# One DMA per block across two batches for x and its reciprocal sums, in a fused attention and two-layer kernel on one Trainium2 core

## The chip, the core and the metric

The kernel runs on one core of one Trainium2 chip as one program. The metric is the time of one execution on the device in microseconds (us), the median over several runs. A profile of one further execution was taken by the hardware profiler. Engines are called PE (matrix products), ACT, DVE and POOL (elementwise work) and SP (which here only issues DMAs).

## The reference, cut to what matters

```python
# q, k, v: 4 batches, 8 heads, 576 positions, 64 wide; x below: 2304 tokens x 512
scores = scale * np.matmul(q, k.transpose(0, 1, 3, 2))
thresh = np.max(scores, axis=-1, keepdims=True) - tau
scores = np.where(scores >= thresh, scores, -1000000000.0)
attn = np.exp(scores - np.max(scores, axis=-1, keepdims=True))
attn = attn / (np.sum(attn, axis=-1, keepdims=True) + 1e-09)
x = heads_side_by_side(np.matmul(attn, v))
g = x @ w_gate                                   # 512 -> 1536
x = (g * (1.0 / (1.0 + np.exp(-g))) * (x @ w_val)) @ w_out
out = ((x @ w1) * (x @ w2) @ w3) @ w_out2        # 512 -> 1024 -> 1024 -> 512
```

## The kernel before

Matrix products are made of two float32 halves: each operand is rounded to a high part (a cast on ACT), a low part is the difference (a subtraction on DVE, helper `sub`, L1545), and three products of the halves (`PASSES`, helper `mm3`, L1505) replace one.

The first stage, attention, goes over 16 pairs of heads (4 batches of 4 pairs). It leaves two things in DRAM. `x_dram` holds the value products, not yet divided by the sums: two partial results (first axis) by 512 features by 4 batches by 576 positions. Each pair of heads stores its 2 x 64 features of a batch (L899, and L1350 for the last two pairs). `r_dram` holds the reciprocals of the softmax sums as high and low halves, for 4 batches and 8 heads (`r_store`, L693 to L702).

The second stage works on 2304 tokens, batch after batch, in five blocks of 512, 512, 256, 512 and 512 columns (`blocks`, numbers 0 to 4). A batch has 576 positions, so blocks 1, 2 and 3 each lie over the end of a batch: block 1 has 64 columns of batch 0 and 448 of batch 1, block 2 has 128 and 128, block 3 has 448 and 64. `segs` cuts a block at these ends. `x_block` (L1846) brings a block in. Its sums come by two DMAs for each piece (L1857), one for each half of the heads. For each of four groups of 128 features (kk) one DMA for each piece (L1871) brings both partial results, POOL adds them (L1879), PE spreads the reciprocals over 128 partitions by a small product with a 0/1 matrix (`spread`, L1887), DVE multiplies (L1895), ACT takes the high half (L1899) and DVE the low half (L1545). Blocks 3 and 4 keep the multiplied value too (ACT, L1904). The spreads of block 0 go to banks `T` (four of one bank each), those of the other blocks to banks `S` (two of two banks each, so two spreads fill one, and the next pair needs the other).

Then `plain` (L1783) makes the first three column groups f of the gate and value products for all blocks, 24 matrix products per block and f on PE (in four groups of three, twice), a silu on ACT (L1806), a multiply on DVE (L1815) and a store of h (L1818). Later groups use a seven-product scheme (`seven`, L1712). Weights are unpacked from 64-bit words beside it (L422, L423 on ACT; L1587, L1590, L1595, L1599, L1601 on DVE).

The end of attention runs in the same span as the start of the second stage: the last pair's probabilities are turned on PE (L587) and split into `AT` and `ATL` by POOL (L367, L372) or by ACT and DVE (L1297, which frees a bank `T` when it is done), and the value products follow (L1327 and L1332, in banks `T`), whose results ACT copies and SP stores.

The order of every engine's instructions is fixed before the run by a planner (`Program.order`, L194). Each step has an engine, how long it keeps it (`busy`), after what time its result is seen (`until`), the buffers that it reads and writes, and a due number. The planner replays all queues with these costs, and of the steps that can start soonest it takes the one with the smallest due number. So a changed cost of one step can change the places of others on all engines. SP's queue is strictly in order: an issue that waits holds all later ones. The costs that `x_block` gives are 1.2 for each piece of the sums and 0.55 for each piece of an x load.

## Time and profile before

| what | value |
|---|---|
| median of 3 runs | 1075.82 us (1075.81, 1075.82, 1083.23) |
| the profiled execution | 1077.25 us |
| its span, from first to last instruction | 1075.5 us |
| instructions | 17044 |
| granted clock of PE, mean | 0.994 of full speed |
| DMA | 162.37 MB, 151 GB/s in the mean |

The profiled execution's time holds its span and 1.75 us around it. The granted clock is at full speed in every stretch that this case is about. The views used below are the busy time by stretch, and the timeline of single engines, in which a row gives the start, the duration (of all instructions that it merges, where xN stands at its end), the engine, the source line, what is written and read, and in brackets how long the engine stood idle before it and which instruction released it.

### The profile page before, as it was taken

To read this page: it belongs to the slowest core of one execution; us is meant where nothing else is said; L and a number is where in the kernel's file an instruction comes from. 1 tells how busy PE (TensorE), PEld (TensorE's weight loads), DVE (VectorE), ACT (ScalarE), POOL (GpSimd) and SP (SyncE) were. 2 spreads that over 40 slices of the span, in tenths; PEclk is the share of its full clock that TensorE was granted. 3 is DMA by queue.
4 is the path that set the end of the run, shared out by engine and by line. 5 is a ranking of instruction groups with operands and counts; after the bars stand their busy time and mean duration, and the time that the engine had idled before them with its cause. 6 is when DMAs were issued, how large, how long until landed. Compare 5 with 4: busy or idle time off the path is not lost.

```text
span 1075.5 us, 17044 instructions
## 1 busy us (share of the span) xinstructions
PE 1046.3 (97%) x5834; PEld 909.8 (85%) x5834; DVE 851.3 (79%) x1680; ACT 632.3 (59%) x1288; POOL 284.7 (26%) x307
## 2 busy tenths in 40 slices
PE   7999999999999999999999999999999999999998
PEld 6898898999977888888888889878888888888886
DVE  7999999999998879999999975976977776442320
ACT  5898898998975546665667654544433444232220
POOL 4799898997865000000000000000000000000000
PEclk8999999999999999999999999999999999999999
DMA  7686867765557124546456661461222325621531
GB/s 181 145 219 166 198 168 176 189 169 145 152 155 252 70 99 159 181 154 204 155 181 238 226 230 41 157 234 40 84 84 89 122 92 193 240 79 53 150 121 49
DMA packets 127206, 162.37 MB, mean 151 GB/s; under 512 B 48688, under 2 KB 83312, under 8 KB 127120
## 3 DMA queue, kind: packets, MB, share of 16 engines
q1 hardware_dynamic: 126976, 161.29, 49.9%
q8 instruction: 46, 0.75, 0.3%
q14 instruction: 40, 0.33, 0.1%
q10 hardware_dynamic: 144, 0.00, 0.0%
HBM read 93.47 MB, written 44.19 MB: 128 GB/s over the span
## 4 chain that ended last, share of the span: by engine, by line
PE 72%; DVE 17%; DMA 3%; issue 3%; ACT 2%; POOL 2%; SPq 1%; DVEq 0%; ACTq 0%; POOLq 0%
PE t_bank L1505 26%; PE t_bank L1705 16%; PE s_bank L1705 11%; PE s_bank L1505 6%; PE s_bank L623 5%; DVE E L655 3%; DVE P L671 3%; PE t_bank L865 3%; PE t_bank L587 3%; DVE slot L1545 3%; POOL AT L372 1%; PE t_bank L877 1%; DVE stat L664 1%; DMA slot<-v_dram 1%; DMA slot<-x_dram 1%
## 5 line engine op out<-in xcount | busy, mean ns | idle before, releaser
L1505 PE MATMUL t_bank<-slot,slot 128*128 128x512 f32 (+1 forms) x1680 | 339.2, 360 | 2.5 <-DVE slot L1545 2.5
L1505 PEld LDWEIGHTS t_bank<-slot,slot 128*128 128x128 f32 x1680 | 284.0, 189 | 53.2 <-DVE slot L1545 4.4
L1705 PE MATMUL t_bank<-slot,slot 128*128 128x512 f32 x816 | 196.7, 390 | 0.9 <-ACT tmp L1724 0.9
L1545 DVE TENSOR_TENSOR slot<-slot,slot 128x512 fp32r<-128x512 f32 (+1 forms) x247 | 157.4, 672 | 40.4 <-ACT slot L1996 27.1
L1705 PEld LDWEIGHTS t_bank<-slot,slot 128*128 128x128 f32 x816 | 152.0, 188 | 32.4 <-ACT tmp L1724 1.6
L1705 PE MATMUL s_bank<-slot,slot 128*128 128x512 f32 x612 | 147.0, 389 | 0.0
L372 POOL TENSOR_TENSOR AT<-tmp,AT 128x512 fp32r<-128x512 f32 x105 | 136.6, 1310 | 3.8
L1705 PEld LDWEIGHTS s_bank<-slot,slot 128*128 128x128 f32 x612 | 114.9, 188 | 23.8
L1724 ACT COPY tmp<-t_bank 128x512 f32<-128x512 f32 x102 | 59.3, 583 | 114.0 <-PE t_bank L1705 113.9
L680 ACT ACTIVATE P<-P,stat 128x576 f32<-128x576 f32 x144 | 113.8, 795 | 6.5 <-DVE P L671 6.3
L671 DVE SCALAR_TENSOR_TENSOR P<-E,stat,s_bank 128x576 f32<-128x576 f32 x144 | 114.4, 809 | 1.7
L1553 ACT CAST slot<-slot 128x512 fp32r<-128x512 f32 x135 | 81.1, 621 | 52.2 <-DVE slot L1545 21.3
L623 PE MATMUL s_bank<-R,L 128*128 128x288 f32 x512 | 95.3, 310 | 12.7 <-DVE P L671 9.9
L655 DVE TENSOR_SCALAR_CACHE_REDUCE E<-s_bank 128x576 f32<-128x576 f32 x135 | 100.5, 753 | 8.1 <-PE s_bank L623 7.3
L623 PEld LDWEIGHTS s_bank<-R,L 128*128 128x128 f32 x512 | 74.6, 191 | 20.8 <-DVE P L671 7.2
L587 PE MATMUL t_bank<-ident,P 128*128 128x128 f32 x640 | 89.1, 274 | 0.5 <-ACT tmp L797 0.2
L1505 PE MATMUL s_bank<-slot,slot 128*128 128x512 f32 (+1 forms) x432 | 84.7, 354 | 0.0
L1505 PEld LDWEIGHTS s_bank<-slot,slot 128*128 128x128 f32 x432 | 71.5, 189 | 11.3
L865 PE MATMUL t_bank<-AT,sp 128*128 128x288 f32 x448 | 76.9, 304 | 0.5 <-POOL AT L372 0.5
L422 ACT ACTIVATE raw<-raw,ebias 128x512 int32<-128x512 int32 x76 | 58.8, 774 | 31.3 <-DVE slot L1595 29.4
L587 PEld LDWEIGHTS t_bank<-ident,P 128*128 128x128 f32 x640 | 74.5, 141 | 3.2 <-ACT tmp L797 0.7
L367 POOL TENSOR_SCALAR AT<-tmp 128x512 fp32r<-128x512 f32 x105 | 66.3, 638 | 31.4 <-ACT tmp L797 26.1
(159 smaller groups left out, 1339.3 us busy)
## 6 DMA issues: line engine op xcount, KB each, us to landing
slot<-h_dram SPq DMA_DIRECT2D x40, 512.0 KB
h_dram<-h SPq DMA_DIRECT2D x34, 512.0 KB
raw<-in_moe_w_dram SPq DMA_DIRECT2D x32, 512.0 KB
raw<-in_moe_w_out_dram SPq DMA_DIRECT2D x20, 512.0 KB
x_dram<-xs SPq DMA_DIRECT2D x64, 144.0 KB
L<-qlo SPq DMA_DIRECT2D x60, 128.0 KB
L<-qhi SPq DMA_DIRECT2D x60, 128.0 KB
raw<-in_moe_w_gate_dram SPq DMA_DIRECT2D x12, 512.0 KB
```

Of the source, the lines that this page charges most:

```text
L367: nc.gpsimd.tensor_scalar(out=hi, in0=src, scalar1=1.0, scalar2=1.0, op0=ALU.mult, op1=ALU.mult)
L372: nc.gpsimd.tensor_tensor(out=lo, in0=src, in1=f32(hi), op=ALU.subtract)
L587: nc.tensor.matmul(bank[:, t * P:(t + 1) * P], lhsT=part, rhs=ident, is_transpose=True, start=(t == 0), stop=(t == len(parts) - 1),)
L623: nc.tensor.matmul(o, lhsT=lhs, rhs=R[:, c:c + HALF], start=(h == hs2[0] and e == 0), stop=(h == hs2[-1] and e == 1),)
L655: nc.vector.tensor_scalar(out=halves(t), in0=sb[:, :, 0:HALF], scalar1=-FAR, scalar2=None, op0=ALU.mult, op1=ALU.min, accum_out=st[:, 0, c],)
L671: nc.vector.scalar_tensor_tensor(out=halves(p_tile(p, i)), in0=halves(t), scalar=st[:, 1, c], in1=sb[:, :, 0:HALF], op0=ALU.is_gt, op1=ALU ...
L680: nc.scalar.activation(out=u, in_=u, func=ACTF.Exp, scale=-FAR, bias=st[:, 0, c], accum_out=sums[p // HP][:, c],)
L865: nc.tensor.matmul(b["t"][:, 0:HALF], lhsT=splits[p, 2][:, 4 * h + c, :, :].rearrange("p a d -> p (a d)"), rhs=AT[h][:, e, c, cs], start=( ...
L1505: nc.tensor.matmul(o, lhsT=lhs(a), rhs=rhs(c), start=(first and i == 0), stop=(last and i == 2))
L1545: nc.vector.tensor_tensor(out=out, in0=x, in1=y, op=ALU.subtract)
L1553: act(lambda: nc.scalar.copy(out=un["t"][:, 0, :], in_=src()), [key], [(un, 0)], 0.52, due, after)
L1705: nc.tensor.matmul(ap(), lhsT=un["t"][:, a, (off + kk) * P:(off + kk + 1) * P], rhs=x[kk]["ap"](c), start=(start and kk == 0 and i == 0), ...
```

## The change

The layout of `r_dram` changes from batch, half and head, position to half and head, batch, position, so that positions of one head run on over the batches, as they do in `x_dram` already. `x_block` then takes a block's columns out of batches and positions as one axis: two DMAs for the sums and one DMA for each kk, whatever batches the block lies in. The steps' costs for the planner are those of one piece for all blocks. Blocks 0 and 4 had one piece before, so for them only the layout of the sums is new.

```diff
--- before.py
+++ after.py
@@ -334,7 +334,7 @@
     ps = ctx.enter_context(tc.tile_pool(name="ps", bufs=1, space=PSUM))
 
     x_dram = dram.tile([2, DM, B, S], F32, name="x_dram")
-    r_dram = dram.tile([B, 2 * H, S], F32, name="r_dram")
+    r_dram = dram.tile([2 * H, B, S], F32, name="r_dram")
     h_dram = dram.tile([NF1, P, NT], F32, name="h_dram")
     h2_dram = dram.tile([NF2, P, NT], F32, name="h2_dram")
     v_dram = dram.tile([NF2 + NF2 // 2, P, 2, 512], F32, name="v_dram")
@@ -692,7 +692,7 @@
 
         def r_store(b, rt):
             for e in range(2):
-                dst = r_dram[b, e * H:(e + 1) * H]
+                dst = r_dram[e * H:(e + 1) * H, b]
                 nc.sync.dma_start(
                     out=dst[:, 0:512].rearrange("h (t c) -> h t c", c=P), in_=f32(rt[0:4 * H, e, :])
                 )
@@ -1848,18 +1848,16 @@
         x_new(j)
         r = buf("hb" if j else "tmp")
         rv = lambda: (r["t"][:, 0, :] if j else r["t"]).bitcast(F32R)
-        pieces = list(segs(c0, n))
-        parts = [b for _, b, _, _ in pieces]
+        parts = [b for _, b, _, _ in segs(c0, n)]
 
         def r_go():
-            for o, b, c, m in pieces:
-                for i in range(2):
-                    nc.sync.dma_start(
-                        out=f32(rv()[32 * i:32 * i + H, o:o + m]),
-                        in_=r_dram[b].rearrange("(e i h) s -> i e h s", e=2, i=2)[i, :, :, c:c + m],
-                    )
-
-        sp(r_go, [("r", b) for b in parts], [(r, 0)], 1.2 * len(pieces), 2.0 + 1.2 * len(pieces), due, after)
+            for i in range(2):
+                nc.sync.dma_start(
+                    out=f32(rv()[32 * i:32 * i + H, 0:n]),
+                    in_=r_dram.rearrange("(e i h) b s -> i e h (b s)", e=2, i=2)[i, :, :, c0:c0 + n],
+                )
+
+        sp(r_go, [("r", b) for b in parts], [(r, 0)], 1.2, 3.2, due, after)
         for k2 in range(2):
             bank = buf("S") if j else None
             for kk in (2 * k2, 2 * k2 + 1):
@@ -1867,14 +1865,14 @@
                 t = buf("slot", F32)
 
                 def load(t=t, kk=kk):
-                    for o, b, c, m in pieces:
-                        nc.sync.dma_start(
-                            out=t["t"][:, :, o:o + m],
-                            in_=x_dram[:, kk * P:(kk + 1) * P, b, c:c + m].rearrange(
-                                "e p c -> p e c"),
-                        )
-
-                sp(load, [("x", b, kk, h) for b in parts for h in range(2)], [(t, 0)], 0.55 * len(pieces), 3.5 + 0.55 * len(pieces), due, after)
+                    nc.sync.dma_start(
+                        out=t["t"][:, :, 0:n],
+                        in_=x_dram[:, kk * P:(kk + 1) * P].rearrange(
+                            "e p b s -> p e (b s)")[:, :, c0:c0 + n],
+                    )
+
+                sp(load, [("x", b, kk, h) for b in parts for h in range(2)], [(t, 0)], 0.55, 4.05,
+                   due, after)
                 xw, wk = whole_ap(j, kk), whole_key(j, kk)
                 prog.add("POOL", size(n, 1.4, 0.8), size(n, 1.45, 0.85), lambda t=t, xw=xw: nc.gpsimd.tensor_tensor(
                     out=xw(), in0=t["t"][:, 0, 0:n], in1=t["t"][:, 1, 0:n], op=ALU.add
```

The changed costs move instructions on all engines in a stretch around the end of attention; PE's order differs in two places only (one spread of block 1 and one pair of spreads of block 2 stand a few places earlier). Lines behind L1866 have numbers that are 2 smaller in the changed kernel, and the loads are its L1855 (sums) and L1868 (x).

SP's queue around the loads of blocks 3 and 4 of x, before. The targets h are the sums' buffers, slot the buffers of x, h_dram the store of a finished h tile; 448 and 64 are the columns of the two pieces.

```order
L1818 DMA h_dram_71<-tmp_5145 128x512
L1857 DMA h_5213<-r_dram_70 8x1x448 x2
L1857 DMA h_5213<-r_dram_70 8x1x64 x2
L1871 DMA slot26_5237<-x_dram_69 128x2x448
L1871 DMA slot26_5237<-x_dram_69 128x2x64
L1818 DMA h_dram_71<-tmp_5201 128x512
L1871 DMA slot27_5259<-x_dram_69 128x2x448
L1871 DMA slot27_5259<-x_dram_69 128x2x64
L1871 DMA slot29_5267<-x_dram_69 128x2x448
L1871 DMA slot29_5267<-x_dram_69 128x2x64
L1871 DMA slot31_5283<-x_dram_69 128x2x448
L1871 DMA slot31_5283<-x_dram_69 128x2x64
```

The same place in the changed kernel; `h_5161` holds the sums of block 3 and `h_5216` those of block 4, and the next store of h stands behind the last row.

```order
L1855 DMA h_5161<-r_dram_70 8x1x512 x2
L1868 DMA slot23_5178<-x_dram_69 128x2x512
L1818 DMA h_dram_71<-tmp_5138 128x512
L1868 DMA slot25_5192<-x_dram_69 128x2x512
L1868 DMA slot26_5198<-x_dram_69 128x2x512
L1868 DMA slot27_5203<-x_dram_69 128x2x512
L1855 DMA h_5216<-r_dram_70 8x1x512 x2
L1868 DMA slot30_5229<-x_dram_69 128x2x512
L1868 DMA slot33_5242<-x_dram_69 128x2x512
L1868 DMA slot34_5246<-x_dram_69 128x2x512
L1868 DMA slot35_5257<-x_dram_69 128x2x512
L1570 DMA raw_5261<-in_moe_w_gate_dram 128x4x256
```

Block 3's seven later DMAs of x became three behind one store, the second store moved behind all loads of block 4, and block 4's loads follow directly.

DVE's order before, at the end of attention, from the first multiplies of block 0 on. `slot8` and `slot9` are block 0, `slot12` is block 1, `AT` the turned probabilities, `rt` the last reciprocals, `raw` a weight being unpacked. Behind the last row three subtractions (L1545) follow, the last of which ends the split of block 0.

```order
L1895 TENSOR_TENSOR slot8_4749<-slot8_4749,t_bank_4938 128x512
L1895 TENSOR_TENSOR slot8_4749<-slot8_4749,t_bank_4951 128x512
L1595 SCALAR_TENSOR_TENSOR slot4_4929<-raw_1252,slot4_4929 128x512
L1451 TENSOR_TENSOR rt_4984<-t_bank_4978,rt_4984 36x128
L1545 TENSOR_TENSOR slot11_4988<-slot8_4749,slot11_4988 128x512
L1297 TENSOR_TENSOR AT_111<-t_bank_4991,AT_111 128x512
L1297 TENSOR_TENSOR AT_111<-t_bank_4998,AT_111 128x512
L1895 TENSOR_TENSOR slot12_5014<-slot12_5014,s_bank_4943 128x512
L1545 TENSOR_TENSOR slot13_5032<-slot8_4749,slot13_5032 128x512
L1599 TENSOR_TENSOR raw_1252<-raw_1252 128x512
L1895 TENSOR_TENSOR slot9_4812<-slot9_4812,t_bank_5053 128x512
L1895 TENSOR_TENSOR slot9_4812<-slot9_4812,t_bank_5057 128x512
```

The same place after. Here `slot11` is block 1; one more multiply of block 0 and three subtractions follow behind the last row, the last of which ends the split of block 0.

```order
L1893 TENSOR_TENSOR slot8_4749<-slot8_4749,t_bank_4941 128x512
L1893 TENSOR_TENSOR slot8_4749<-slot8_4749,t_bank_4953 128x512
L1893 TENSOR_TENSOR slot11_4956<-slot11_4956,s_bank_4945 128x512
L1451 TENSOR_TENSOR rt_4980<-t_bank_4977,rt_4980 36x128
L1545 TENSOR_TENSOR slot12_4984<-slot8_4749,slot12_4984 128x512
L1595 SCALAR_TENSOR_TENSOR slot7_4932<-raw_1252,slot7_4932 128x512
L1297 TENSOR_TENSOR AT_111<-t_bank_4987,AT_111 128x512
L1297 TENSOR_TENSOR AT_111<-t_bank_4994,AT_111 128x512
L1545 TENSOR_TENSOR slot13_5027<-slot8_4749,slot13_5027 128x512
L1545 TENSOR_TENSOR slot14_5031<-slot11_4956,slot14_5031 128x512
L1893 TENSOR_TENSOR slot11_4956<-slot11_4956,s_bank_4945 128x512
L1893 TENSOR_TENSOR slot9_4812<-slot9_4812,t_bank_5051 128x512
```

A multiply of block 1 moved ahead of the two L1297, L1595 moved behind the first subtraction, a subtraction of block 1 came in, and L1599 moved out behind the three subtractions.

POOL's order before, from the end of one split of `AT` on; the L1879 are adds of block 1 (128x512) and then of block 2 (128x256).

```order
L372 TENSOR_TENSOR AT_111<-tmp_4851,AT_111 128x512
L367 TENSOR_SCALAR ATL_112<-tmp_4973 128x512
L372 TENSOR_TENSOR ATL_112<-tmp_4973,ATL_112 128x512
L1879 TENSOR_TENSOR slot12_5014<-slot10_4911 128x512
L367 TENSOR_SCALAR AT_111<-tmp_5029 128x512
L372 TENSOR_TENSOR AT_111<-tmp_5029,AT_111 128x512
L1879 TENSOR_TENSOR slot12_5014<-slot5_4946 128x512
L1879 TENSOR_TENSOR slot16_5079<-slot6_4964 128x512
L1879 TENSOR_TENSOR slot16_5079<-slot7_4981 128x512
```

And after:

```order
L372 TENSOR_TENSOR AT_111<-tmp_4851,AT_111 128x512
L1877 TENSOR_TENSOR slot11_4956<-slot10_4889 128x512
L367 TENSOR_SCALAR ATL_112<-tmp_4973 128x512
L372 TENSOR_TENSOR ATL_112<-tmp_4973,ATL_112 128x512
L1877 TENSOR_TENSOR slot11_4956<-slot4_4907 128x512
L367 TENSOR_SCALAR AT_111<-tmp_5025 128x512
L372 TENSOR_TENSOR AT_111<-tmp_5025,AT_111 128x512
L1877 TENSOR_TENSOR slot15_5056<-slot5_4913 128x512
L1877 TENSOR_TENSOR slot15_5056<-slot6_4920 128x512
```

The first add of block 1 moved ahead of the split of `ATL`, and the rest moved up by one.

## Rows read from the trace of the kernel before

**Rows 1.** The page, busy time, share of the span and instructions of each engine

```profile
PE 1046.3 (97%) x5834; PEld 909.8 (85%) x5834; DVE 851.3 (79%) x1680; ACT 632.3 (59%) x1288; POOL 284.7 (26%) x307
```

**Rows 2.** Busy us (instructions) by stretch: PE, PEld, DVE, ACT, POOL

```profile
315.00:320.00 5.00, 3.90 (x19) 2.74 (x19) 5.00 (x5) 1.70 (x4) 3.97 (x3) 1.00 0.37 82
...
350.00:375.00 25.00, 25.00 (x129) 21.38 (x128) 21.97 (x39) 14.12 (x25) 0.00 (x0) 1.00 0.19 68
```

**Rows 3.** Timeline of PE

```profile
305.34 0.49 PE L1887 MATMUL t_bank<-tmp,pick 8*128 8x512 f32 x1 [0.42 <-DVE AT L1297]
...
310.80 1.33 PE L1327 MATMUL t_bank<-AT,sp 128*128 128x288 f32 x8
...
317.89 0.96 PE L1505 MATMUL t_bank<-slot,slot 128*128 128x512 f32 x3 [0.38 <-DVE slot L1545]
319.58 4.83 PE L1505 MATMUL t_bank<-slot,slot 128*128 128x512 f32 x20 [0.73 <-DVE slot L1545]
...
335.16 0.73 PE L1887 MATMUL s_bank<-h,pick 8*128 8x512 f32 x2
...
338.77 0.73 PE L1887 MATMUL s_bank<-h,pick 8*128 8x512 f32 x2
...
343.16 0.73 PE L1887 MATMUL s_bank<-h,pick 8*128 8x512 f32 x2 [0.72 <-DVE slot L1545]
...
346.94 0.73 PE L1887 MATMUL s_bank<-h,pick 8*128 8x512 f32 x2 [0.71 <-DVE slot L1545]
```

**Rows 4.** Timeline of SP's queue

```profile
297.85 2.57 SPq L1857 DMA_DIRECT2D h<-r_dram  x4
...
326.67 2.49 SPq L1857 DMA_DIRECT2D h<-r_dram  x4
329.20 0.91 SPq L1871 DMA_DIRECT2D slot<-x_dram  x2
333.51 0.33 SPq L1818 DMA_DIRECT2D h_dram<-tmp  x1
333.94 2.98 SPq L1871 DMA_DIRECT2D slot<-x_dram  x6
```

**Rows 5.** Timeline of POOL

```profile
308.00 1.59 POOL L372 TENSOR_TENSOR ATL<-tmp,ATL 128x512 fp32r<-128x512 f32 x1
309.56 1.75 POOL L1879 TENSOR_TENSOR slot<-slot 128x512 f32<-128x512 f32 x1
...
313.74 5.23 POOL L1879 TENSOR_TENSOR slot<-slot 128x512 f32<-128x512 f32 x3
...
333.25 1.30 POOL L1879 TENSOR_TENSOR slot<-slot 128x512 f32<-128x512 f32 x1 [4.90 <-DMA slot<-x_dram]
338.30 1.28 POOL L1879 TENSOR_TENSOR slot<-slot 128x512 f32<-128x512 f32 x1 [3.75 <-DMA slot<-x_dram]
```

**Rows 6.** Timeline of DVE

```profile
303.81 0.41 DVE L1587 TENSOR_SCALAR slot<-raw 128x512 int32<-128x512 int32 x1
...
307.62 0.84 DVE L1595 SCALAR_TENSOR_TENSOR slot<-raw,slot 128x512 f32<-128x512 uint16 x1
...
308.58 1.56 DVE L1545 TENSOR_TENSOR slot<-slot,slot 128x512 fp32r<-128x512 f32 x1
310.07 1.27 DVE L1297 TENSOR_TENSOR AT<-t_bank,AT 128x512 fp32r<-128x512 f32 x2
...
315.45 4.07 DVE L1545 TENSOR_TENSOR slot<-slot,slot 128x512 fp32r<-128x512 f32 x3
...
323.65 0.96 DVE L1587 TENSOR_SCALAR slot<-raw 128x512 int32<-128x512 int32 x1
...
339.78 0.69 DVE L1545 TENSOR_TENSOR slot<-s_bank,slot 128x512 fp32r<-128x512 f32 x1 [1.14 <-ACT slot L1904]
340.57 1.51 DVE L1895 TENSOR_TENSOR s_bank<-slot,s_bank 128x512 f32<-128x512 f32 x2
```

**Rows 7.** Timeline of ACT

```profile
341.30 0.59 ACT L1899 CAST slot<-s_bank 128x512 fp32r<-128x512 f32 x1 [1.05 <-DVE s_bank L1895]
```

## The prediction

> **What bounds the kernel now.** I read the page's busy table first: PE is busy 1046.3 us of a span of 1075.5 us [rows 1], so all idle time of PE in the whole run is 29.2 us, and a change that leaves PE's work alone can bring no more. The change touches loads that are issued between about 298 and 341 us, so the second view is the busy time by stretch there. What the reader is to see: PE lacks 1.10 us between 315 and 320, and nothing between 350 and 375 [rows 2]. From 350 on PE is fed while its order of work stays the same, so the value of this change is the shift in the moment at which PE leaves the stretch before. The third view, PE's timeline, has the waits in their places: 0.42 us at 305.34, 0.38 at 317.89, 0.73 at 319.58, 0.72 at 343.16 and 0.71 at 346.94, four of the five for L1545, the subtraction that makes the low half of a split block [rows 3]. Their sum, 2.96 us or 0.28% of the time, is the most that the change can give back. A measurement of this kernel can tell about 1%, 10.8 us, from no change, so the whole question lies inside that bound.
>
> The first three waits belong to blocks 0 and 1, the last two to the spreads of block 4 (L1887), which need a bank that block 3 still holds.
>
> **The change part by part.** It removes 6 loads of reciprocal sums (16 become 10) and 12 loads of x (32 become 20). On SP's queue four loads of sums took 2.57 us, 0.64 each, and six of x 2.98 us, 0.50 each [rows 4]: 6 x 0.64 + 12 x 0.50 = 9.8 us of queue time. SP isn't the bound, so this is worth only what then arrives earlier on PE's path. The same bytes go into the same tiles. No work of PE, ACT, DVE or POOL is added or removed; the planner's smaller costs reorder some of it.
>
> *Blocks 3 and 4.* Before, SP issued the first x load of block 3 at 329.20, then stood behind a store of h that went at 333.51, and sent the other six pieces from 333.94 [rows 4]. POOL waited 4.90 us for the first and 3.75 us for the second [rows 5]. In the new order the only h store inside these loads is the first one, and in the trace block 3's sums were sent right behind that store, at 326.67 [rows 4]. So the three remaining loads of block 3 go at about 326.7 instead of 333.94, 7.2 us earlier; 3 x 0.50 and 2 x 0.64 later, at 329.5, the loads of block 4 follow. From the issue at 329.20 to the add at 333.25 is 4.05 us [rows 4, 5]; with that, block 3's adds can run at 327 to 332 and block 4's by 338.
>
> What is late next is PE's own order: block 3's first spread stands behind products that end at 335.16 [rows 3]. From the spread's end, 335.9, the bank must pass two multiplies of 0.75 us and a subtraction of 0.69 us on DVE [rows 6] and two casts and two copies of 0.59 us on ACT [rows 7]: the first multiply ends at 336.6, the four steps of ACT at 339.0, the last subtraction near 339.7. PE wants the bank at 343.16 - 0.72 = 342.44, so 2.7 us are left. The second bank, spread at 338.77, is free near 343.3, and PE wants it at 346.94 - 0.72 - 0.71 = 345.5, so 2.2 us are left [rows 3]. Both waits go: **-1.43 us**. If that cover is gone, because block 3's data still lands late, the cost is those 1.43 us again, and no more.
>
> *Blocks 0 and 1.* Two sum loads fewer put the first x load of block 1 at 297.85 + 2 x 0.64 = 299.1 [rows 4], and all four go before the next store. Landing after 4.05 us, the first add can start at about 303.2. This is the add that the planner put ahead of the split of ATL; it lasts 1.3 us alone and 1.75 us beside DVE, so it is over by 305.0, 3 us before the second half of that split at 308.00 [rows 5]. The gain: one add fewer in the three that took 5.23 us from 313.74 [rows 5], beside which three subtractions took 4.07 us on DVE, against 3 x 0.69 = 2.07 us [rows 6]. The price: DVE works beside the moved add at 303.8, and its bit mask L1587, 0.41 us there, took 0.96 us beside a later add [rows 6], so +0.55 us. And DVE's order changes: a multiply of block 1 (0.75 us) now stands in front of the pair of L1297 that frees banks for the value products, and L1595 has moved from ahead of the subtraction of 308.58 to behind it, where POOL starts its next add. Low end: L1595 keeps its 0.84 us [rows 6], and the pair comes 0.55 + 0.75 = 1.3 us later. High end: L1595 is held for a whole add of 1.75 us, 0.9 more, 2.2 us in all. I take 1.9, nearer to the high end, since L1545 in that place was held to the end of POOL's instruction. The second value product started at 310.80 [rows 3], when the first L1297 of 310.07 was just over [rows 6], so it has no slack: PE waits there up to 1.9 us, and comes as much later to the first products of block 0.
>
> But there PE waited 0.38 + 0.73 us anyway for the last subtractions of block 0 [rows 3], and what decides is when the last of those ends. Counted on from the pair's end, near 313.2: two subtractions held beside POOL's split and add (to 316.0), a multiply (316.7), two more (318.0), three subtractions back to back (some 320.0, or 319.7 if they overlap as the three L1545 at 0.6 from start to start do). The trace has 315.45 + 4.07 = 319.52 for that end [rows 6], and PE's fourth group at 319.58 [rows 3]. The late pair and the lighter end cancel to within some tenths: I take **0 us**, between -1.1 (both waits gone) and +2.2 (all of the pair's delay arrives at PE).
>
> Here a rule of the Trainium skill speaks against the change. SBUF — State Buffer, section "SBUF: two separate sides", says that a DVE instruction with two SBUF inputs and a GpSimd instruction that reads SBUF shut each other out for a whole instruction. The trace agrees for L1545: at 308.58 it took 1.56 us and ended 0.55 us after POOL's instruction of 308.00 did [rows 5, 6]. If the rule holds for the moved L1595 too, the pair is late by the high end, 2.2 us; by L1595's own row, 0.84 us while POOL also worked, it is late by the low end, 1.3 us.
>
> **Sum.** 0 - 1.43 = -1.43 us. The profiled execution took 1077.25 us, a span of 1075.5 and 1.75 around it; with the change it would take 1075.8. The median of the runs is 1075.82, 1.43 below the profiled execution, so the same difference puts the median at 1074.4 us.
>
> **The rivals.**
>
> Slower: POOL's add, moved next to DVE's work, delays the bank-freeing pair, and the end of block 0 doesn't win it back. Place: DVE from 303.8 to 313. Price: 2.2 us at PE, less 1.43 later, +0.8 us, 1076.6 us. It decides from the point where more than 1.43 us of DVE's delay reach PE's fourth group at 319.58. For it speaks that the second value product has no slack [rows 3, 6]; against it, that POOL has one add less at the end.
>
> Gain on both sides: DVE ends block 0 early enough that all five waits go, -2.96 us, 1072.9 us. For it speaks the 2.0 us that the three subtractions lost beside POOL; against it the longer list in front of them.
>
> Nothing gained: the merged loads land no sooner, since the bytes are the same, or block 4's spreads find the bank held by ACT and DVE as before. PE leaves the stretch at the same moment: 1075.8 us. POOL's two long waits [rows 5] speak against it, as they follow the late issue and not the transfer; ACT's 1.05 us of waiting for DVE's multiply at 341.30 [rows 7] speaks for a chain that is long even with data there.
>
> **How the numbers follow.** The forecast gets 0.48, the slower rival 0.20, the large gain 0.20, no effect 0.12. The range runs from the large gain, 1072.9, with a tenth for the spread of the runs, 1072.8, to the slower rival, 1076.6; some 2 in 10 are left for what lies outside these sums. No case comes near 1% of the time: the largest gain is 2.96 us and the largest loss 2.2 us against 10.8 us. So faster by over 1% gets 0.02, slower by over 1% 0.02, for something outside these views, and within 1% gets 0.96.
>
> **What would show it.** Right: PE's waits for L1545 in front of L1887 after 340 us are gone, POOL's waits for block 3's x fall from four to five us to under two, the three later x loads of block 3 go near 327, and PE is without a gap from about 320 on. The first stretch is right if a PE wait appears before the second value product near 311 and the fourth group of L1505 starts within 0.5 us of 319.6. Wrong: a new wait of PE after 350, the fourth group later than 321, block 4's spreads waiting still, or L1595 at about 0.8 us in its new place, which would take the slower rival away.

## The result, and the profile after

| | before | after |
|---|---|---|
| median | 1077.24 us (20 runs, 1075.81 to 1089.82) | 1085.59 us (20 runs, 1082.53 to 1089.68) |
| ratio | 1 | 1.006, 95% interval 1.004 to 1.008 |
| profiled execution, span | 1077.25, 1075.5 us | 1082.89, 1081.2 us |
| PE busy | 1046.3 us | 1048.8 us |

The change made the kernel slower by 0.6%: inside the band of 1% that the prediction named, but 9 us above the top of its range. Of before's 20 runs 12 lie at 1076 to 1078 us and seven at 1081 to 1086, so the ratio isn't that of the two medians (1.0078); the means, 1079.39 and 1085.87 us, give 1.0060. The last section shows one place where some 5 us can be lost, in attention, which the change doesn't touch. The ratios of the experiments leave out one execution of run 3 (3197.66 us) and one of run 4 (1096.19 us), which took far longer than the others of their kernel; the profile of run 4 is of that one and is not used.

So the traces are compared from one moment on, the second spread of block 0 in a bank `T`: 305.34 us before, 305.37 after. Up to the second spread of block 4, which is called the stretch from here on, PE has nearly the same work to do, and takes **41.60 us before** (to 346.94 [rows 3]) and **47.47 us after** (to 352.84): 5.87 us more, while the profiled executions differ by 5.64. From there to the end of the span the two take 728.56 and 728.36 us.

PE's timeline after, in that stretch (start, duration of all merged instructions, engine, line; in brackets the idle time before and its releaser). Line numbers after the change are 2 lower from the x loads on: the spread is L1885, the multiply L1893, the cast L1897, the copy L1902.

```profile
304.02 0.46 PE L1885 MATMUL t_bank<-tmp,pick 8*128 8x512 f32 x1 [1.15 <-ACT ATL L1428]
...
305.37 0.50 PE L1885 MATMUL t_bank<-tmp,pick 8*128 8x512 f32 x1 [0.42 <-DVE AT L1297]
...
309.26 2.77 PE L587 MATMUL t_bank<-ident,P 128*128 128x128 f32 x12
...
318.36 5.63 PE L1505 MATMUL t_bank<-slot,slot 128*128 128x512 f32 x24
...
336.10 0.73 PE L1885 MATMUL s_bank<-h,pick 8*128 8x512 f32 x2
...
340.37 3.01 PE L1505 MATMUL t_bank<-slot,slot 128*128 128x512 f32 x12
347.55 1.22 PE L1885 MATMUL s_bank<-h,pick 8*128 8x512 f32 x2 [4.17 <-ACT slot L1902]
...
352.84 1.08 PE L1885 MATMUL s_bank<-h,pick 8*128 8x512 f32 x2
```

Three things answer to [rows 3]. The waits of 0.38 and 0.73 us in front of block 0's products are gone (24 products run on from 318.36 without a gap), yet block 3's first spread comes at 336.10 instead of 335.16, 0.94 later. The wait in front of block 4's first spread has grown from 0.72 to 4.17 us, +3.45. And from that spread to the next it takes 352.84 - 347.55 = 5.29 us instead of 343.16 to 346.94 = 3.78, although the wait of 0.71 us in it has gone. 0.94 + 3.45 + 1.51 = 5.90 us.

The busy time by stretch says why the same work takes longer (the column PEclk is the granted clock):

```profile
core 0: us, PE busy (x) PEld busy (x) DVE busy (x) ACT busy (x) POOL busy (x), PEclk, DMA share, GB/s
300.00:306.00 6.00, 4.33 (x30) 3.27 (x28) 5.79 (x15) 3.89 (x10) 3.08 (x3) 0.99 1.00 382
306.00:312.00 6.00, 5.48 (x23) 4.83 (x24) 5.21 (x10) 3.60 (x7) 3.57 (x3) 0.50 0.04 10
...
347.00:353.00 6.00, 5.45 (x21) 4.58 (x21) 3.95 (x7) 3.24 (x6) 0.00 (x0) 0.50 0.01 4
```

After PE stood idle for 1.15 and 0.42 us, and again after the 4.17 us, the granted clock was 0.50 in a row of six microseconds each, which is the lower level, 1.2 of 2.4 GHz. In before it was 1.00 in all these rows. The spread pair took 1.22 instead of 0.73 us there, and 12 transposes of L587 2.77 instead of 1.47. A lower clock raises PE's busy time: the row of 347 to 353 has PE at work for 5.45 of 6 us, and 21 matrix products in it where before has 40.

The timelines of SP, POOL and DVE after, parts of each:

```profile
324.93 0.36 SPq L1868 DMA_DIRECT2D slot<-x_dram  x1
328.91 0.34 SPq L1818 DMA_DIRECT2D h_dram<-tmp  x1
329.30 1.49 SPq L1868 DMA_DIRECT2D slot<-x_dram  x3
...
332.12 1.96 SPq L1868 DMA_DIRECT2D slot<-x_dram  x4
```

```profile
333.14 4.40 POOL L1877 TENSOR_TENSOR slot<-slot 128x512 f32<-128x512 f32 x3 [1.70 <-DMA slot<-x_dram]
337.71 6.28 POOL L1877 TENSOR_TENSOR slot<-slot 128x512 f32<-128x512 f32 x4 [0.17 <-DMA slot<-x_dram]
```

```profile
302.05 1.18 DVE L1480 TENSOR_TENSOR marks<-ident 40x4 f32<-40x4 f32 x1
...
310.24 1.75 DVE L1595 SCALAR_TENSOR_TENSOR slot<-raw,slot 128x512 f32<-128x512 uint16 x1
311.92 1.27 DVE L1297 TENSOR_TENSOR AT<-t_bank,AT 128x512 fp32r<-128x512 f32 x2
...
317.31 2.45 DVE L1545 TENSOR_TENSOR slot<-slot,slot 128x512 fp32r<-128x512 f32 x3
...
330.20 1.79 DVE L1599 TENSOR_TENSOR raw<-raw 128x512 int32<-128x512 int32 x1
...
338.12 1.78 DVE L1601 SCALAR_TENSOR_TENSOR slot<-slot,raw 128x512 f32<-128x512 f32 x1
340.59 1.01 DVE L1545 TENSOR_TENSOR slot<-slot,slot 128x512 fp32r<-128x512 f32 x1 [0.69 <-ACT slot L1553]
341.52 0.68 DVE L1815 TENSOR_TENSOR tmp<-tmp,t_bank 128x512 f32<-128x512 f32 x1
342.12 1.48 DVE L1893 TENSOR_TENSOR s_bank<-slot,s_bank 128x512 f32<-128x512 f32 x2
344.74 0.69 DVE L1545 TENSOR_TENSOR slot<-s_bank,slot 128x512 fp32r<-128x512 f32 x1 [1.14 <-ACT slot L1897]
```

The loads do come earlier, as meant: block 3's three later ones at 329.30 instead of 333.94, block 4's at 332.12, and POOL's waits of 4.90 and 3.75 us [rows 5] are down to 1.70 and 0.17. But block 3's multiplies, for which all this was to be in time, stand at 342.12; its spread was done at 336.8. In front of them DVE unpacks a weight pair (L1587 to L1601) beside POOL's adds, and single instructions (L1599, L1601) take 1.78 to 1.79 us that took 0.68 and 0.69 before, at 328.56 and 329.27. The bank is given back at 347.5 by the copy of L1902, and PE has waited for it since 343.38.

### The profile page after: what moved, and what is told of

The parts are those of the page before. It is cut to its first block, busy times and chain, and to the rows that moved or that the text cites. A ratio compares the mean times of both kernels' runs of the same rounds, so it can differ in the third digit from the quotient of the medians.

```text
span 1081.2 us, 17016 instructions
## 1 busy us (share of the span) xinstructions
PE 1048.8 (97%) x5834; PEld 912.9 (84%) x5834; DVE 854.7 (79%) x1680; ACT 634.0 (59%) x1288; POOL 284.9 (26%) x307
## 4 chain that ended last, share of the span: by engine, by line
PE 73%; DVE 17%; issue 2%; ACT 2%; DMA 2%; POOL 2%; SPq 1%; DVEq 0%; ACTq 0%; POOLq 0%
PE t_bank L1505 26%; PE t_bank L1705 16%; PE s_bank L1705 11%; PE s_bank L1505 6%; PE s_bank L623 5%; PE t_bank L865 3%; PE t_bank L587 3%; DVE P L671 3%; DVE slot L1545 3%; DVE E L655 3%; DVE raw L1599 1%; PE t_bank L877 1%; DVE slot L1601 1%; DVE slot L1595 1%; DVE stat L664 1%
## 5 line engine op out<-in xcount | busy, mean ns | idle before, releaser
L1545 DVE TENSOR_TENSOR slot<-slot,slot 128x512 fp32r<-128x512 f32 (+1 forms) x247 | 156.6, 670 | 40.7 <-ACT slot L1994 26.5
L623 PE MATMUL s_bank<-R,L 128*128 128x288 f32 x512 | 94.4, 308 | 12.8 <-DVE P L671 10.0
L587 PE MATMUL t_bank<-ident,P 128*128 128x128 f32 x640 | 92.3, 280 | 0.5 <-ACT tmp L797 0.2
L623 PEld LDWEIGHTS s_bank<-R,L 128*128 128x128 f32 x512 | 73.6, 189 | 20.8 <-DVE P L671 7.1
L587 PEld LDWEIGHTS t_bank<-ident,P 128*128 128x128 f32 x640 | 77.4, 144 | 3.3 <-ACT tmp L797 0.7
```

Source lines behind the costliest of these rows:

```text
L587: nc.tensor.matmul(bank[:, t * P:(t + 1) * P], lhsT=part, rhs=ident, is_transpose=True, start=(t == 0), stop=(t == len(parts) - 1),)
L623: nc.tensor.matmul(o, lhsT=lhs, rhs=R[:, c:c + HALF], start=(h == hs2[0] and e == 0), stop=(h == hs2[-1] and e == 1),)
L1545: nc.vector.tensor_tensor(out=out, in0=x, in1=y, op=ALU.subtract)
```

## The experiments

Theory: early adds on POOL hold DVE's unpacking; in the new order that unpacking stands in front of block 3's multiplies; so block 3's bank comes back late, PE idles and its clock falls. Rivals: the order alone, the merged transfers alone, or the early gap at 303 us with the lower clock after it. The changed kernel has two parts, the DMAs and the order that follows from the planner's costs; the first two runs are one without the other.

**1. Merged loads, costs and order of before; 2. loads by pieces, costs and order of after.** The edit of run 1 in the changed kernel (the cost of the x loads likewise); run 2 is the reverse edit in the kernel before.

```diff
-        ..., 1.2, 3.2, due, after)
+        ..., 1.2 * len(parts), 2.0 + 1.2 * len(parts), due, after)
```

> The merged loads of the changed kernel, with the planner's costs of before, so that PE, DVE, ACT and POOL stand in the order of before and only SP's queue is new. Theory A (the new order of the engines is what costs): within 2 us of the kernel before, 1075 to 1078 us, with PE's waits for block 4's spreads not above the 0.72 and 0.71 us of before. Theory B (the earlier data is what costs, as POOL's adds then stand beside DVE's work): slower than before by 4 us or more, 1081 us and up, with DVE's unpacking held beside the adds between 325 and 345 us.

> The loads in pieces of before, with the planner's costs of the changed kernel, so that all engines stand in the order of the changed kernel but each piece has its own DMA. Theory A (order): as slow as the changed kernel or slower, 1083 to 1090 us, with a wait of several us in front of a spread of block 4. Theory B (earlier data): within 2 us of the kernel before, since the pieces come late again.

Measured: 1.0008 [0.9980, 1.0036] and 1.0003 [0.9980, 1.0026]. Neither part alone costs anything that can be told from nothing; both together cost 0.6%. The stretch says it more clearly: 42.45 and 42.86 us, against 41.60 before and 47.47 after. So both theories fall, and the loss is an interaction of the two parts. Run 1 is no test of an earlier block 3, though: in the order of before its three later loads still stand behind a store of h and go at 334.25. Run 2 has the changed kernel's order on every engine, so its DVE can be laid beside that of the changed kernel. Groups of instructions on DVE from 324 to 342 us (busy us, mean ns), first after, then run 2:

```profile
L1599 DVE TENSOR_TENSOR raw<-raw 128x512 int32<-128x512 int32 x2 | 3.2, 1618 | 0.0
...
L1601 DVE SCALAR_TENSOR_TENSOR slot<-slot,raw 128x512 f32<-128x512 f32 x2 | 2.5, 1232 | 0.0
L1815 DVE TENSOR_TENSOR tmp<-tmp,t_bank 128x512 f32<-128x512 f32 x3 | 2.0, 676 | 0.0
L1595 DVE SCALAR_TENSOR_TENSOR slot<-raw,slot 128x512 f32<-128x512 uint16 x2 | 1.9, 954 | 0.0
...
L1587 DVE TENSOR_SCALAR slot<-raw 128x512 int32<-128x512 int32 x2 | 1.4, 686 | 0.0
```

```profile
L1815 DVE TENSOR_TENSOR tmp<-tmp,t_bank 128x512 f32<-128x512 f32 x3 | 2.0, 680 | 0.0
L1599 DVE TENSOR_TENSOR raw<-raw 128x512 int32<-128x512 int32 x2 | 1.6, 789 | 0.0
L1601 DVE SCALAR_TENSOR_TENSOR slot<-slot,raw 128x512 f32<-128x512 f32 x2 | 1.6, 775 | 0.0
...
L1595 DVE SCALAR_TENSOR_TENSOR slot<-raw,slot 128x512 f32<-128x512 uint16 x2 | 1.4, 684 | 0.0
...
L1587 DVE TENSOR_SCALAR slot<-raw 128x512 int32<-128x512 int32 x2 | 0.8, 422 | 0.0
```

L1599, L1601, L1595 and L1587 lose 1.6 + 0.9 + 0.5 + 0.6 = 3.6 us; L1815, which reads one operand from a PSUM bank, is the same in both. In run 2 block 3's first multiply starts at 337.95, and PE's waits for block 4 are 0.86 and 1.57 us.

**3. The 0/1 matrix made early, in the changed kernel; 4. the same in run 1's kernel.** After the change the matrix's first step, L1480, takes 1.18 us beside the moved add, and PE waits 1.15 us. The profile names ACT's L1428 for that wait, but it was over at 303.50; the matrix's last step ended at 303.92, and the spread started at 304.02.

```diff
-            for step in steps:
+            for n, step in enumerate(steps):
+                if n == len(steps) // 2:
+                    make_pick()
...
-    dve(make_pick, [], [("pick", 0)], 0.5, -34.0)
+    dve(lambda: None, [], [("pick", 0)], 0.5, -34.0)
```

> The changed kernel, with the 0/1 matrix for the spreads made halfway through attention and its planned step left empty. Theory A1 (POOL's moved add holds the making of this matrix on DVE, 1.18 us against 0.14, PE stands idle for 1.15 us before the first spread, and its clock falls to the lower level at 306 us): the gap at 303 us shrinks to under 0.5 us, no fall of the clock between 305 and 313 us, first products of block 0 earlier by 2 to 3 us, in all 2 to 4 us faster than the changed kernel. Rival (the gap waits for the bank that ACT frees, or the clock falls anyway): no change beyond 1 us.

> The first kernel of this set with the 0/1 matrix made halfway through attention as well. If POOL's add does not stand beside the making of the matrix in the old order, nothing changes against the first kernel (within 1 us). If the matrix also delays the first spread there, up to 0.5 us faster, or more if a fall of the clock near 306 us goes with it.

Measured: 1.0082 [1.0051, 1.0113] and 1.0029 [1.0004, 1.0053]. In run 3 the gap at 303 us and the lower clock behind it are gone, and a wait of 3.15 us in front of block 4's spread stays: the jam doesn't need the early gap. The time is no better. What the gap costs by itself the run doesn't show, for the edit has a price of its own in attention, where the matrix's steps now take 1.26, 1.12 and 1.33 us beside POOL's work at 146.4 to 150.2 and PE waits for what stands behind them:

```profile
151.26 0.77 PE L623 MATMUL s_bank<-R,L 128*128 128x288 f32 x4 [2.90 <-issue]
```

The stretch is 44.67 us, 2.80 less than after, so the early gap may hold a part of the loss.

**5. POOL's adds for blocks 2 to 4 cut to 128 columns.** One partial result of x is loaded straight to where the sum goes, and the other is left out, so this kernel computes something else.

```diff
+                    if j > 1:
+                        nc.sync.dma_start(out=into(), in_=x_dram[0, ...][:, c0:c0 + n])
+                        return
...
-                    out=xw(), in0=t["t"][:, 0, 0:n], in1=t["t"][:, 1, 0:n], op=ALU.add
+                    out=xw()[:, 0:128], in0=xw()[:, 0:128], in1=xw()[:, 0:128], op=ALU.add
```

> The changed kernel with POOL's twelve adds for blocks 2, 3 and 4 cut from 512 (or 256) columns to 128; every engine's order is that of the changed kernel. The computation is changed: of x for these blocks only the first partial result is loaded, straight into the tile that the add wrote, and POOL adds only 128 columns of it to themselves. Theory (POOL's earlier adds hold DVE's two-input unpacking at 324 to 341 us, so block 3's multiplies stand at 342.12 instead of 337.95, and PE idles 4.17 us in front of block 4's spread, with the lower clock behind it): DVE's L1587, L1595, L1599 and L1601 in that stretch fall back to 0.41, 0.69, 0.69 and 0.68 us, block 3's first multiply starts near 338, the 4.17 us become at most 1.2, the granted clock stays full behind them, and the time is within 0.3% of the kernel before (1075 to 1082, ratio 0.997 to 1.003). Rival 1 (it is the new order's bank handling of ACT and DVE, not the held unpacking): the wait stays above 3 us, ratio 1.004 to 1.008. Rival 2 (the early gap at 303 us and the lower clock after it carry the loss): the wait at 347 goes, yet the ratio stays at 1.004 or more.

Measured: 1.0019 [0.9995, 1.0043]. PE and DVE of this run (line numbers are 8 higher):

```profile
345.07 0.73 PE L1893 MATMUL s_bank<-h,pick 8*128 8x512 f32 x2
...
349.68 0.73 PE L1893 MATMUL s_bank<-h,pick 8*128 8x512 f32 x2 [1.53 <-ACT slot L1910]
```

```profile
330.81 0.68 DVE L1599 TENSOR_TENSOR raw<-raw 128x512 int32<-128x512 int32 x1
...
336.87 0.89 DVE L1601 SCALAR_TENSOR_TENSOR slot<-slot,raw 128x512 f32<-128x512 f32 x1
...
339.66 1.47 DVE L1901 TENSOR_TENSOR s_bank<-slot,s_bank 128x512 f32<-128x512 f32 x2
```

The wait of 4.17 us is gone altogether, the clock from 325 on is full, and from block 0's second spread (307.01) to block 4's second it is 42.67 us instead of 47.47. The order is that of the changed kernel, the gap of 1.14 us at 305 is still there, and so is the lower clock after it: rivals 1 and 2 of this run fall. It also moves half the bytes of x, so by itself it doesn't part POOL's work from the transfers; run 9 does.

**6. Each add in pieces of 128 columns.**

```diff
-nc.gpsimd.tensor_tensor(out=xw(), in0=t["t"][:, 0, 0:n], ...)
+[nc.gpsimd.tensor_tensor(out=xw()[:, o:o + 128], in0=t["t"][:, 0, o:o + 128], ...)
+ for o in range(0, n, 128)]
```

> The changed kernel with each of POOL's adds in x_block split into instructions of 128 columns (two or four in place of one), same order otherwise. Theory (a two-input instruction of DVE is held until POOL's running instruction ends): no hold can be longer than one short add of about 0.4 us, so L1599 and L1601 fall from 1.8 us to 1.1 or less, block 3's first multiply comes at 338.5 to 341, the wait in front of block 4's spread falls from 4.17 to between 1 and 3 us, ratio to the kernel before 1.000 to 1.004. Rival (what DVE loses is set by POOL's total time, not by the length of one instruction): the holds only break up into more and shorter ones, with the same sum, the multiply stays near 342 and the ratio at 1.005 or more, since more instructions make POOL's adds longer in all.

In the trace the theory holds: L1599 and L1601 take 0.68 to 0.95 us, the wait is 1.21 us, and the stretch 43.91 us. The time was 1.0060 [1.0033, 1.0086], no better. By its ratio the rival was right, by its trace not. The profile doesn't explain that: the stretch's gain is there, and its execution reached block 0's second spread only at 312.19 us, in the main for what the last section shows. Why the median of these 12 runs stays high is open.

**7. Pieces for blocks 3 and 4 only; 8. pieces for blocks 0 to 2 only**, both in the changed kernel's order. The edit of run 7; in run 8 the condition is `j < 3`, and the sums are cut likewise.

```diff
-                    nc.sync.dma_start(out=t["t"][:, :, 0:n], in_=...)
+                    for o, b, c, m in segs(c0, n) if j > 2 else [(0, None, c0, n)]:
+                        nc.sync.dma_start(out=t["t"][:, :, o:o + m], in_=...)
```

> The changed kernel, its order on every engine kept, but blocks 3 and 4 loaded by pieces again (block 3: four loads of sums and eight of x instead of two and four; block 4 has one piece anyway). Theory (adds that come early meet the unpacking): block 3's adds come 1 to 3 us later than in the changed kernel, but block 2's still early, so part of the holds stays: wait in front of block 4's spread 1.5 to 3.5 us, ratio 1.001 to 1.005. Rival (the harm is done by block 3's own loads alone): as with all loads by pieces in this order, wait 0.9 to 1.6, ratio 0.998 to 1.002. Rival 2 (the harm is done by blocks 0 to 2): unchanged, 4.2 us and 1.006.

> The changed kernel, its order on every engine kept, but blocks 0, 1 and 2 loaded by pieces again and only blocks 3 and 4 merged. Theory: SP reaches block 3's loads some 3 to 6 us later than in the changed kernel (323.58 there), so the adds of blocks 2 and 3 fall near where they fell with all loads by pieces, DVE's unpacking runs mostly free, the wait in front of block 4's spread is 0.9 to 2.5 us, ratio 0.998 to 1.003. Rival (the merged loads of block 3 do harm in this order wherever they stand): wait above 3 us and ratio 1.004 to 1.008.

Measured: 1.0034 [1.0011, 1.0058] with a wait of 3.93 us and 46.54 us for the stretch, and 1.0033 [1.0008, 1.0058] with waits of 1.20 and 1.57 and 43.87 us. The times don't part them, the traces do, by the place of block 3's first multiply in the table below. Merging blocks 0 to 2 moves it by 3.0 us (32.78 to 35.82 with block 3 in pieces, 33.79 to 36.75 with it merged), merging block 3 by 1.0 us (32.78 to 33.79, 35.82 to 36.75). So the early blocks' shorter queue makes most of the jam; run 7's wait, above the 1.5 to 3.5 us of its theory, is nearly that of its rival 2. In run 7 block 2's adds hold DVE's masks at 325 to 329 us (L1587 once 0.96, L1590 twice 0.85), and block 3's later adds meet the L1601 that stands just ahead of the multiplies, which takes 0.68 us in that place in run 2 (and 1.77 in run 8):

```profile
337.09 1.78 DVE L1601 SCALAR_TENSOR_TENSOR slot<-slot,raw 128x512 f32<-128x512 f32 x1
```

**9. The unpacking moved behind block 3; 10. that, and the matrix early; 11. the same move in the kernel before; 12. the changed kernel again.**

```diff
-    unit_pair(raws_left[1:3], (("g", 2), ("v", 2)), None, room[1], due=0.0, step=0.7)
...
     x_block(3, 0.0, room[1])
+    unit_pair(raws_left[1:3], (("g", 2), ("v", 2)), None, room[1] + [prog.steps[-1]], due=0.0, step=0.7)
```

> The changed kernel with its merged loads and costs; the unpacking of one weight pair (two each of L1587, L1590, L1595, L1599, L1601 and the low halves that go with them) is tied to block 3's last step and so moves behind block 3's multiplies on DVE. PE's and POOL's orders stay. Theory (early adds hold the unpacking, and the unpacking holds block 3's multiplies): with nothing of two inputs in SBUF beside the adds, block 3's first multiply starts right after its spread, some 31 us after the second spread of block 0 instead of 36.75, the 4.17 us in front of block 4's spread are gone (under 0.5), the clock stays full behind them, and from block 0's second spread to block 4's second spread it takes 41 to 43 us instead of 47.47: ratio to the kernel before 0.997 to 1.002. Rival (block 3's bank takes 5.4 us a bank in the new order of ACT and DVE, whatever stands in front): waits of 1 to 2 us remain, ratio 1.002 to 1.005. Rival 2 (the unpacking only moves the jam to 350 to 380 us): a new wait of PE there, ratio over 1.004.

> As the run with the unpacking behind block 3, and the 0/1 matrix for the spreads made halfway through attention instead of next to POOL's add at 303 us. Theory: both PE gaps that the changed kernel has of its own are gone, the clock is full from 300 to 375, and 0.5 to 1.5 us come off the other run: ratio 0.996 to 1.001. Rival (as in the run with the early matrix alone, the gap only moves to the pair of L1297, 1.3 us, and the matrix costs attention time): no gain on the other run or up to 2 us more, ratio 1.000 to 1.004.

> The kernel before, loads by pieces, with the same unpacking moved behind block 3. Theory: in the kernel before the multiplies of block 3 stand only 0.6 us behind what they could, since its adds come late; the move frees little, PE's waits of 0.72 and 0.71 us go or stay: ratio 0.997 to 1.001. If it gains as much against the kernel before as the move gains on the changed kernel (0.4% or more), the move is a gain by itself and no evidence about the merged loads.

> The changed kernel once more, beside the others on this chip: ratio 1.004 to 1.009, and in its profile the same wait of 3.5 to 4.5 us in front of block 4's first spread with the granted clock at its lower level behind it, some 47 us from block 0's second spread to block 4's second. If the profile lies 2 to 4 us higher in time than the first one, where PE stands longer shows what the median holds beyond the 5.9 us seen there; if the time lies in attention, before 300 us, it is not of the loads' making alone.

Measured: run 9 1.0023 [1.0000, 1.0045], run 10 1.0041 [1.0018, 1.0064], run 11 1.0016 [0.9991, 1.0042], run 12 1.0049 [1.0032, 1.0067]. PE in run 9 and in run 12:

```profile
349.90 0.73 PE L1885 MATMUL s_bank<-h,pick 8*128 8x512 f32 x2
...
353.62 0.72 PE L1885 MATMUL s_bank<-h,pick 8*128 8x512 f32 x2 [0.64 <-ACT slot L1902]
...
359.29 0.73 PE L1505 MATMUL t_bank<-slot,slot 128*128 128x512 f32 x2 [1.16 <-ACT slot L1553]
360.40 24.95 PE L1505 MATMUL t_bank<-slot,slot 128*128 128x512 f32 x120 [0.39 <-DVE slot L1545]
```

```profile
347.17 1.22 PE L1885 MATMUL s_bank<-h,pick 8*128 8x512 f32 x2 [4.42 <-ACT slot L1902]
348.32 3.94 PE L1505 MATMUL t_bank<-slot,slot 128*128 128x256 f32 x18
352.18 0.73 PE L1885 MATMUL s_bank<-h,pick 8*128 8x512 f32 x2
```

Run 9 keeps all bytes, all adds and the early loads, and the jam is gone: 41.53 us for the stretch. The adds meet DVE's multiplies, which read a PSUM bank, and cost them nothing. But the moved weights are now late themselves and cost PE 1.16 + 0.39 us at 359, which the stretch doesn't show; its ratio is just above its theory's 1.002, and beside run 12's on the same chip it is not told apart by the times alone. Run 11 says that the move is no gain by itself: in the kernel before it brings the first multiply 1.95 us forward and makes the second wait 1.65 us. Run 12 has the jam again, 4.42 us and 47.17 for the stretch, with the lower clock behind it (18 products in 3.94 us, 2.42 in run 9). Run 10 has the shortest stretch of all, 40.79 us, but the early matrix costs it the same 2.90 us of waiting in attention (at 151.34) as run 3, and its ratio is at the upper end of its rival's. No version was faster than the kernel before.

| run | first multiply of block 3, from block 0's second spread | waits before block 4's spreads | stretch, us | ratio |
|---|---|---|---|---|
| 11, unpacking behind, in before | 30.66 | 0, 1.65 | 42.48 | 1.0016 |
| 10, unpacking behind, matrix early | 30.70 | 0, 0.64 | 40.79 | 1.0041 |
| 9, unpacking behind | 31.44 | 0, 0.64 | 41.53 | 1.0023 |
| before | 32.61 | 0.72, 0.71 | 41.60 | 1 |
| 5, short adds | 32.65 | 0, 1.53 | 42.67 | 1.0019 |
| 2, pieces, order of after | 32.78 | 0.86, 1.57 | 42.86 | 1.0003 |
| 1, merged, order of before | 33.46 | 1.23, 0.72 | 42.45 | 1.0008 |
| 8, pieces for 0 to 2 | 33.79 | 1.20, 1.57 | 43.87 | 1.0033 |
| 6, split adds | 33.82 | 1.21, 1.57 | 43.91 | 1.0060 |
| 3, matrix early | 34.59 | 3.15, 0 | 44.67 | 1.0082 |
| 7, pieces for 3 and 4 | 35.82 | 3.93, 0 | 46.54 | 1.0034 |
| 12, after again | 36.72 | 4.42, 0 | 47.17 | 1.0049 |
| after | 36.75 | 4.17, 0 | 47.47 | 1.006 |

From 33.5 us on, the later block 3's multiplies, the longer the first wait (but for runs 1, 8 and 6, which are alike) and the stretch, whichever edit set their place. The ratio doesn't follow: runs 3 and 10 lose 2.90 us in attention, and run 6's profiled execution some 5 us there. So the runs show where the 5.87 us of the stretch come from, and not the whole of the loss.

## Why the prediction was wrong

**Bound and measure: right.** PE's feed in 298 to 353 us decides, from there on the two take the same time, and the result is within 1%.

**Loads earlier: right in kind.** Block 3's three later loads went at 329.30, not at 326.7: the h store ahead of them waited for its multiply, L1815, to 328.9. POOL's long waits for block 3's x went.

**Blocks 3 and 4, -1.43 us: the step that failed.** It was "From the spread's end, 335.9, the bank must pass two multiplies ...: the first multiply ends at 336.6". That took DVE to be free at 335.9, and the bank's path to last 3.8 us from there (to 339.7). Both were wrong. The first multiply started at 342.12, 6.2 us later. DVE's order was read at 303 to 320 us and not at this place, where in the new order an L1601, an L1545 and an L1815 stand right in front of the multiplies and most of the unpacking before these; and POOL's adds, which the step itself had moved there ("block 3's adds can run at 327 to 332 and block 4's by 338"), held it. In run 2, in the new order with few holds, the multiply came at 337.95: about 2 us of the lateness are not the holds', 4 are. Those 2 us could be read in the trace of the kernel before, where the multiply stands at 337.95 too, though its add was over at 334.55 [rows 5]:

```profile
337.35 0.68 DVE L1815 TENSOR_TENSOR tmp<-tmp,t_bank 128x512 f32<-128x512 f32 x1
337.95 0.69 DVE L1895 TENSOR_TENSOR s_bank<-slot,s_bank 128x512 f32<-128x512 f32 x1
```

And the bank's path took 5.38 us, from 342.12 to 347.50, not 3.8: ACT's two copies and DVE's two subtractions waited for each other in turn (0.81, 0.71 and 0.81 us), where the prediction ran ACT's four steps without a break.

```profile
346.91 0.59 ACT L1902 COPY slot<-s_bank 128x512 f32<-128x512 f32 x1 [0.81 <-DVE slot L1545]
```

The 2.05 us of a later start and the 1.6 of a longer path alone are more than the margin of 2.7: run 2 waits 0.86. With the holds, in place of two waits that go, 0.72 + 0.71, there is one of 4.17.

**The lower clock: not in the sum at all.** "If that cover is gone ... the cost is those 1.43 us again, and no more" took a wait to cost its length. The 4.17 us brought 5.29 us for work that took 3.07 before (3.78 less the wait of 0.71): 2.2 us on top.

**Blocks 0 and 1, 0 us between -1.1 and +2.2: in its bounds, in part by luck.** The pair of L1297 came at 311.92 instead of 310.07, 1.85 us later where 1.9 was taken, but the terms were others. L1595 in its new place took 1.75 us, exactly the high end. L1587 at 303.85 was not held (0.41), since the moved add ran from 301.94 to 303.21 already and met L1480 instead; and DVE stood idle for 0.52 and 0.24 us, which no term had. Block 0's last subtraction ended at 319.76, where 319.7 was said. The sign named for it, a PE wait before the second value product, is in run 2 (1.29 us at 312.01) but not after the change, where PE itself came there later, at the lower clock. PE reached block 3's first spread 0.94 us later than before. In run 2, in the same order at full clock, that spread came 30.08 us behind block 0's second spread, against 29.82 before and 30.73 after; so most of the 0.94 us goes with the lower clock from 306 to 312, which no step had asked for. That clock doesn't need the wait of 1.15 us: in run 8, whose only wait there is 0.42 us, it was 0.57 in the mean of the same row.

**The slower rival was the nearest, in the wrong place.** POOL's adds beside DVE's work were its mechanism, and the price was looked for at 303 to 313 us alone. The page of the Trainium skill that was cited there, SBUF — State Buffer, section "SBUF: two separate sides", was applied to one instruction; the same rule bears on every instruction with two SBUF inputs beside a moved add. The traces agree with it: L1599 1618 ns in the mean beside the adds against 789, L1815 with one PSUM input 676 against 680, and with adds of a quarter length (run 6) no L1599 or L1601 was over 0.95 us.

The 5.64 us between the profiled executions don't hold all of the 8.35 between the medians; the changed kernel's profiled execution is the second fastest of its 20 runs. Where its other runs lose more is open: no profile shows them, but their mean granted clock falls as their time grows, from 0.993 (1082.53 us) to 0.986 (1089.68 us). Run 12's ratio is 1.0049.

## What to carry to other kernels

When a change brings a transfer forward, follow the engine that consumes it to its new time and lay its instructions beside the other engines' there: an add that was harmless at one time can hold another engine's two-input work at another. Read a margin from the new order of the engine that frees the buffer, with all that stands ahead of it, not from the moment at which its data are there, and add up the path of the buffer with the waits of the engines for each other that the trace shows. And where PE waits for several microseconds, read the granted clock behind the wait, for the wait's length was here only two thirds of its price.

## What the runs showed of the hardware

A one-input mask of DVE was held too: L1587 took 0.96 us beside an add in the changed kernel, as it did before [rows 6], and 0.42 in run 2. Which instruction an add meets differs between executions of one kernel: L1480, of 40x4 elements, took 1.18 us in the first profile of the changed kernel and 0.15 in that of run 12, where a mask right behind it, L1590, took 1.39 instead.

A PE gap of about 1.4 us in attention, of the same code in all kernels, was followed by the lower clock in some executions and not in others. The row of the wait and the granted clock behind it, in the kernel before and then in run 6:

```profile
128.04 0.80 PE L623 MATMUL s_bank<-R,L 128*128 128x288 f32 x4 [1.38 <-DVE P L671]
```

```profile
128.00:134.00 6.00, 5.96 (x46) 5.89 (x47) 5.93 (x15) 5.21 (x14) 6.00 (x7) 1.00 0.80 189
```

```profile
128.07 0.80 PE L623 MATMUL s_bank<-R,L 128*128 128x288 f32 x4 [1.43 <-DVE P L671]
141.78 0.77 PE L623 MATMUL s_bank<-R,L 128*128 128x288 f32 x4 [2.41 <-DVE P L671]
```

```profile
128.00:134.00 6.00, 5.93 (x34) 5.93 (x35) 4.68 (x11) 4.31 (x11) 6.00 (x7) 0.72 0.74 187
```

With the clock at 0.72 in the mean, 34 matrix products instead of 46 went through in six microseconds; a second gap of 2.41 us followed, and L623's row of 146.62 in the kernel before stood at 152.06. Run 9's profile has the same (1.41, then 2.41), the changed kernel's first profile has 1.42 and full clock. That is 5 us between executions of the same code, as much as the whole change. Whether the slower runs of one kernel lose their time there no profile shows; they do come with a lower mean granted clock (the kernel before, measured again beside runs 9 to 12: 1.000 at 1074.67 us, 0.990 at 1084.46).
